# Two-layer memory attention with a SwiGLU feed-forward: GpSimd's weight sums of chunk 1, second token pair, without the wait for a copied column

## The chip, the cores and the metric

The kernel runs on one core of a Trainium2 chip. The core has engines that run at the same time, each with its own queue that is worked off in order: TensorE (PE in the profile, with its weight loads as PEld) multiplies matrices into PSUM; VectorE (DVE) and ScalarE (ACT) work element by element on SBUF and PSUM; GpSimd (POOL) does so on SBUF; SyncE (SP) issues the DMA transfers. An instruction whose operands are not ready holds up everything behind it on its engine. The metric is device time in microseconds of one execution of the whole program.

## The reference

The input x has 2048 tokens of width 512. Two layers run one after the other with the same weights. A layer is

```
x = x + A(layernorm(x))      # 32 heads of 16, four segments of 512 tokens; causal softmax attention
                             # in the segment, mixed by a gate with a linear-attention memory of the past segments
x = x + B(layernorm(x))      # B(y) = (silu(y @ w_gate) * (y @ w_up)) @ w_down, inner width 1792
```

All of it is in float32. The change touches B alone, the feed-forward part, and there only the products with w_gate and w_up.

## The kernel before, in words

*Precision.* A float32 matrix is split into a high half, which TensorE's float32 multiply takes exactly (a ScalarE copy that casts), and a low half, the rest (a subtraction). A product of two matrices is three products: high times high, low times high, high times low. So each operand that TensorE reads needs one ScalarE cast and one subtraction on VectorE or GpSimd.

*Tiling of the feed-forward.* The inner width is cut into 7 chunks of 256 (NF = 7). The 2048 tokens are four blocks of 512; the first pair of blocks is m = 0, the second m = 1. For each pair, chunk 0 is computed in the ordinary way (`up`, L1017). Chunks 1 to 6 use Strassen's method with seven products in place of eight (`strassen`, L1047), for gate (g) and up (u). It needs sums of token halves and sums of weight quarters. `down` (L1091, added to x by VectorE at L1096) multiplies the gated result by w_down. The products of gate and up are joined by `gate` and `finish` (L998, L1001, L1003, L1004).

*Token sums.* Once per pair, `make_t(m)` forms four combinations TT[0] to TT[3] of the normalised tokens, each in two k halves (kc = 0, 1), on VectorE (L961); each is split by a ScalarE cast (L982) and a VectorE subtraction (L983). The last index of a TT tile's low half, TT[2], kc = 1, is written late in that chain. The profile names its scratch tiles tt, of and xn, and the results s, which is the name of all the large SBUF slots.

*Weight sums.* `load_s(c, nm)` loads the two raw 128x512 blocks of a chunk's gate or up weights into the ring of four raw tiles phik and phiq (DMA, L858), forms four sums S1 to S4 on GpSimd (L900, 128x256 each) in the scratch tiles mem, and then splits raw quarters and sums into the weight tiles: four ScalarE casts (L913) and four GpSimd subtractions (L914), of 256, 512, 512 and 512 columns. `load_d(c)` does the same for w_down (L865, L867), without sums. Two sets of weight tiles are used in turn, so the casts of a set wait until TensorE has read the set before the last one.

*The order of the work.* The program is not issued as written. Every operation gets a priority (`at(v)`, a due time in steps of the feed-forward) and its dependencies. `Program.issue` then walks through a model of the engines: each engine takes, of the operations that are ready by the model, the one with the lowest due time. The result is one fixed order of instructions per engine. At m = 1 the due time of `load_s(1, "u")` is step 14.1 and that of `load_s(2, "g")` 14.4, those of the pair's layer norms 10.7 and 11.7, and that of `make_t(1)` 28.5.

*The turn.* `pool_turn` makes GpSimd copy one column (128x1) of a tile that another engine writes (L921). The copy waits for that writer. The GpSimd operations of a `load_s` that are given this copy as an extra dependency come behind it in the order. For chunks 2 to 6 the column is one of the gated result of block 1 of the pair. For chunk 1 of the first pair there is none. For chunk 1 of the second pair it is the last column of TT[2]'s low half, kc = 1. The list `turn` is passed to `load_s(c, "u")`, to `load_s(c + 1, "g")`, and to the last GpSimd subtraction of `load_d(c)`.

Of the kernel before, what the change touches and what calls it, by code (L numbers as in the profile page):

```python
# [253 lines left out]
def infini_swiglu(ctx: ExitStack, tc: tile.TileContext, x, wq, wk, wv, wo, beta, wg, wu, wd, out,  # L254
# [11 lines left out]
    def sb(tag, shape, dtype=F32, ring=1):  # L266
        return P.buf(pool, tag, shape, dtype, ring)
# [20 lines left out]
    def gp(cost, fn, reads, writes):  # L288
        op("pool", cost, fn, reads, writes)
# [557 lines left out]
    def ffn(base, x_in, x_out, slots, T):  # L847


        X, XT, TT, Wg, Wd = {}, {}, {}, {}, {}  # L850

        def at(v):
            P.prio = base + v * T
# [28 lines left out]
        def load_gu(tags):  # L882
            for nm, w, tag in zip("gu", (wg, wu), wset()):
                wt = Wg[0, nm] = sb(tag, [128, 2, KC, 256], F32R)
                for kp in range(2):
                    load_part(wt, kp, wsrc(w, 0, kp), tags)
# [31 lines left out]
        def pool_turn(view, read):  # L918

            one = sb("turn", [128, 1], ring=2)  # L920
            gp(0.1, lambda: nc.gpsimd.tensor_copy(one.ap, view().bitcast(F32)), [read], [one])  # L921
            return P.ops[-1:]

        def load_d(c, tags, pool=False):
            wt = Wd[c] = sb(slots[f"d{nd[0] % 2}"], [128, 2, 2, 512], F32R)
            nd[0] += 1
            for fi in range(2):
                r0 = c * 256 + fi * 128
                load_part(wt, fi, wd[r0:r0 + 128, :].rearrange("p (k f) -> p k f", k=1), tags, pool)

        def ln(b):
            XT[b] = (sb(slots[f"H{b % 2}"], TX, F32R), sb(slots[f"L{b % 2}"], TX, F32R))
            for t in range(4):
                xt = sb("xin", [128, 512], ring=2)
                load_rows(xt, x_in, b * 512 + t * 128)
                ln_transpose(ln_norm(xt, lambda a: a, None, XN2), XT[b][0], XT[b][1], t)

        def load_x(b):
            X[b] = sb(slots[f"X{b}"], [128, 4, 512])
            for t in range(4):  # L940
                r0 = b * 512 + t * 128
                dma(lambda t=t, r0=r0: nc.sync.dma_start(X[b].ap[:, t, :], rows(x_in, r0, 128)),
                    dep(x_in, r0 // 128), [(X[b], t)])
# [56 lines left out]
        def finish(sg, sv, ht, fi, pu, ru):  # L1000
            dve(512, lambda: nc.vector.tensor_mul(sv(), sv(), pu()), [sg, ru], [sg])  # L1001
            hv = lambda a: ht.ap[:, 0:2048].rearrange("p (f a c) -> p f a c", f=2, a=2)[:, fi, a]
            act(512, lambda: nc.scalar.copy(hv(0), sv()), [sg], [(ht, (fi, 0))], sbuf=True)  # L1003
            dve(512, lambda: nc.vector.tensor_sub(hv(1), sv(), hv(0).bitcast(F32)),  # L1004
                [sg, (ht, (fi, 0))], [(ht, (fi, 1))])

        def up(b, fi, ht, early):
            res = []
            for nm in "gu":
                ps = bank("pj" if early else ("plt_0", "plt_1", "plt_2", "ppv_0")[nup[0] % 4])  # L1010
                nup[0] += 1
                cs = slice(fi * 128, (fi + 1) * 128)
                first = len(P.ops)
                wt = Wg[0, nm]
                seq = [(i, j, kc) for i, j in ((0, 0), (1, 0), (0, 1)) for kc in range(KC)]
                for x, (i, j, kc) in enumerate(seq):
                    pe(512, 1, lambda i=i, j=j, kc=kc, x=x, ps=ps, wt=wt: nc.tensor.matmul(  # L1017
                        ps.ap, lhsT=wt.ap[:, i, kc, cs], rhs=XT[b][j].ap[:, :, kc], start=(x == 0),
                        stop=(x == len(seq) - 1)), [(wt, (i, kc // 2)), XT[b][j]], [ps])
                if early:  # L1020
                    P.ops[first].deps |= set(last[-1:])
                    last.append(P.ops[-1])
                res.append(ps)
            pg, pu = res
            sg = sb("raw" if early else SG, [128, 512])
            gate(sg, lambda: sg.ap, lambda: pg.ap, pg)
            finish(sg, lambda: sg.ap, ht, fi, lambda: pu.ap, pu)
# [56 lines left out]
        def down(c, b, ht):  # L1084
            for t in range(4):
                ps = bank("pj")
                cs = slice(t * 128, (t + 1) * 128)
                wt = Wd[c]
                seq = [(i, j, fi) for i, j in ((0, 0), (1, 0), (0, 1)) for fi in range(2)]
                for x, (i, j, fi) in enumerate(seq):  # L1090
                    pe(512, 1, lambda i=i, j=j, fi=fi, x=x, ps=ps, wt=wt, cs=cs: nc.tensor.matmul(  # L1091
                        ps.ap, lhsT=ht.ap[:, 0:2048].rearrange("p (f a c) -> p f a c", f=2, a=2)[:, fi, j, cs],
                        rhs=wt.ap[:, i, fi, :], start=(x == 0), stop=(x == len(seq) - 1)),
                       [(wt, (i, fi)), (ht, (fi, j))], [ps])
                xb = X[b]
                dve(512, lambda ps=ps, t=t: nc.vector.tensor_add(xb.ap[:, t, :], xb.ap[:, t, :], ps.ap),  # L1096
                    [ps, (xb, t)], [(xb, t)])
                if c == NF - 1:
                    r0 = b * 512 + t * 128
                    dma(lambda t=t, r0=r0: nc.sync.dma_start(rows(x_out, r0, 128), xb.ap[:, t, :]), [(xb, t)],  # L1100
                        [(x_out, r0 // 128)] if isinstance(x_out, Buf) else [])
# [27 lines left out]
        for m in range(2):  # L1129
            v = m * PAIR  # L1130
            if m:
                at(v - 3.0)
                load_gu(RAW)
                load_d(0, RAW)
                for b in (2, 3):
                    at(v + b - 2 - 1.2)
                    ln(b)
                    at(v + b - 2 - 1.5)
                    load_x(b)
                at(v - 0.66)  # L1140
                down(NF - 1, 0, hts[0])
                at(v + 0.33)
                down(NF - 1, 1, hts[1])
                for b in range(2):
                    hts[b] = hbuf(1 - b)
                    for fi in range(2):
                        at(v + b + 0.5 * fi)
                        up(b + 2, fi, hts[b], False)
            at(v + WAT)
            load_s(1, "g")  # L1150
            at(v + TAT[m])
            make_t(m)
            pend = (0, 1) if m else (1,)
            for c in range(1, NF):
                v = m * PAIR + 2 + (c - 1) * STEP
                at(v)
                gs = strassen(c, "g", m)
                at(v + 0.2)
                if c > 1:
                    turn = pool_turn(lambda ht=hts[1]: ht.ap[:, 1023:1024], (hts[1], (0, 1)))  # L1160
                elif m == 0:
                    turn = []
                else:
                    turn = pool_turn(lambda t=TT[2]: t.ap[:, 1, 3, 1, 127:128], (TT[2], (1, 1)))
                at(v + 0.25)
                load_s(c, "u", turn)
                if c + 1 < NF:
                    at(v + 0.55)
                    load_s(c + 1, "g", turn)
                at(v + 0.8)  # L1170
                load_d(c, RAW, True)
                P.ops[-1].deps |= set(turn)
                end = m == 1 and c == NF - 1 and not isinstance(x_out, Buf)
                before = hts
                for part in ("ud" if end else "du"):
                    at(v + (0.6 if part == "d" and not end else 1.2))
                    if part == "d":
                        for b in pend:
                            down(c - 1, b + 2 * m, before[b])
                    else:  # L1180
                        hts = {b: sb(slots[f"X{b}"], [128, 4 * 512], F32R) if end else hbuf(1 - b) for b in range(2)}
                        us = strassen(c, "u", m)
                        at(v + FIN)
                        for e in ((0, 0), (1, 1), (1, 0), (0, 1)):
                            finish(gs[0][e], gs[1][e], hts[e[1]], e[0], us[1][e], us[0][e])
                pend = (0, 1)
# [61 lines left out]
```

## Time and profile before

| | us |
|---|---|
| three runs | 1876.71, 1881.82, 1885.32 |
| their median | 1881.82 |
| the profiled execution | 1878.99 |
| its span in the profile | 1877.2 |
| TensorE busy | 1825.3 |
| VectorE busy | 1407.5 |
| GpSimd busy | 918.9 |
| ScalarE busy | 873.1 |

The profiled execution is one run of its own. Its span is the time from the first to the last instruction that the profiler recorded. Times in the profile's rows count from the start of the span. In a row of a timeline the first two numbers are the start and the duration in us, then come the engine, the line of the kernel, the operation, the tiles written and read, the shapes and the count; a bracket at the end gives the idle time of the engine before it and what ended it. A row of the windows begins with the stretch and its length and then gives the busy time and the number of instructions of PE, PEld, DVE, ACT and POOL, the clock granted to TensorE as a share of full speed, the mean busy share of the DMA engines, and GB/s.

### The profile page before, as it was taken

The numbers are of one execution on the slowest core, as the hardware profiler recorded it, in microseconds if no ns is written. First come the engines' busy times: TensorE is split into PE (matmuls) and PEld (weight loads), VectorE is DVE, ScalarE is ACT, GpSimd is POOL, SyncE is SP. The second block draws the span as 40 slices with busy tenths as digits, with TensorE's granted clock in tenths as the row PEclk, the third lists the DMA queues.
The fourth block names the chain that finished last, engine by engine and source line by source line (L and its number), as shares of the span: only waits on it lengthen the run. The fifth ranks groups of instructions, "written<-read, shape, count | busy, mean of one in ns | idle before, by whom it ended". The sixth has DMA issues, their size and how long they took to land.

```text
span 1877.2 us, 33021 instructions
## 1 busy us (share of the span) xinstructions
PE 1825.3 (97%) x11360; PEld 1450.6 (77%) x11360; DVE 1407.5 (75%) x3834; ACT 873.1 (47%) x1629; POOL 918.9 (49%) x1186
## 2 busy tenths in 40 slices
PE   7999999999999999999989999999999999999999
PEld 5787787877778887788867877778777788878887
DVE  6878788778876678766776777787898766796656
ACT  4565564555533432433345655556454433333432
POOL 6344444444655654647533444444446647445551
PEclk9999999999999999999999999999999999999999
DMA  7535444464232132111373353455642311312121
GB/s 236 148 102 147 135 133 144 144 214 119 74 119 61 46 91 89 52 50 57 114 217 101 106 163 115 130 167 140 188 124 74 123 51 56 94 64 57 44 58 45
DMA packets 126967, 206.14 MB, mean 110 GB/s; under 512 B 14160, under 2 KB 52048, under 8 KB 126800
## 3 DMA queue, kind: packets, MB, share of 16 engines
q1 hardware_dynamic: 124752, 203.49, 36.7%
q8 instruction: 91, 1.49, 0.3%
q10 hardware_dynamic: 2048, 0.53, 0.1%
q14 instruction: 76, 0.62, 0.1%
HBM read 136.34 MB, written 67.11 MB: 108 GB/s over the span
## 4 chain that ended last, share of the span: by engine, by line
PE 48%; DVE 7%; issue 2%; DMA 2%; POOL 1%; ACT 1%; SPq 0%; DVEq 0%; POOLq 0%; ACTq 0%
PE ps L1047 18%; PE ps L1091 10%; PE ps L295 7%; PE ps L636 3%; PE ps L558 3%; PE ps L609 3%; DVE junk L564 2%; DMA s<-nm 1%; PE ps L1017 1%; DVE tt L961 1%; DVE s L983 1%; DVE s L1096 1%; PE ps L387 1%; DVE mx L564 0%; DVE of L961 0%
## 5 line engine op out<-in xcount | busy, mean ns | idle before, releaser
L1047 PE MATMUL ps<-s,s 128*128 128x512 f32 x2016 | 547.3, 396 | 9.5 <-ACT s L982 4.6
L295 PE MATMUL ps<-s,s 128*128 128x512 f32 x1536 | 526.2, 407 | 2.7 <-ACT s L451 1.2
L564 DVE CUSTOM_DVE_ANT_0 junk<-ps,amask 128x128 bf16<-128x128 f32 (+3 forms) x1024 | 433.5, 484 | 46.5 <-PE ps L558 45.1
L1047 PEld LDWEIGHTS ps<-s,s 128*128 128x128 f32 x2016 | 376.7, 188 | 106.0 <-ACT s L982 6.7
L1091 PE MATMUL ps<-s,vt 128*128 128x512 f32 x1296 | 378.0, 397 | 2.2 <-ACT vt L1003 2.2
L295 PEld LDWEIGHTS ps<-s,s 128*128 128x128 f32 x1536 | 287.2, 191 | 51.6 <-issue 6.1
L615 ACT ACTIVATE s<-ps 128x512 f32<-128x512 f32 x448 | 253.9, 609 | 108.5 <-PE ps L609 97.2
L1091 PEld LDWEIGHTS ps<-s,vt 128*128 128x128 f32 x1296 | 245.2, 189 | 58.6 <-ACT vt L1003 2.6
L558 PE MATMUL ps<-ck,s 127*128 127x256 f32 (+2 forms) x1024 | 276.6, 334 | 5.7 <-DMA ck<-scrk 4.9
L609 PE MATMUL ps<-s,ck 128*128 128x256 f32 x1280 | 250.6, 287 | 6.4 <-DMA s<-nm 4.5
L609 PEld LDWEIGHTS ps<-s,ck 128*128 128x128 f32 x1280 | 221.3, 189 | 38.3 <-issue 4.9
L1096 DVE TENSOR_TENSOR s<-s,ps 128x512 f32<-128x512 f32 x224 | 150.1, 683 | 92.0 <-PE ps L1091 91.7
L619 POOL TENSOR_SCALAR_AFFINE_SELECT s<-s 128x512 f32<-128x512 f32 x192 | 126.8, 663 | 171.9 <-ACT s L615 166.6
L558 PEld LDWEIGHTS ps<-ck,s 127*128 127x128 f32 x1024 | 177.6, 189 | 28.8 <-issue 6.4
L914 POOL TENSOR_TENSOR s<-mem,s 128x512 fp32r<-128x512 f32 x96 | 130.7, 1362 | 0.0
L492 POOL TENSOR_SCALAR s<-raw 128x512 fp32r<-128x512 f32 x64 | 45.4, 709 | 173.9 <-ACT raw L491 163.6
L1017 PE MATMUL ps<-s,s 128*128 128x512 f32 x384 | 123.9, 400 | 0.9 <-ACT s L391 0.9
L921 POOL COPY turn<-vt 128x1 f32<-128x1 f32 x20 | 3.7, 186 | 235.6 <-DVE vt L1004 235.6
L636 PE MATMUL ps<-s,vt 128*32 128x384 f32 (+3 forms) x1536 | 115.7, 419 | 0.1
L636 PEld LDWEIGHTS ps<-s,vt 128*32 128x32 f32 x1536 | 43.3, 109 | 64.1 <-issue 46.2
L615 ACT ACTIVATE pc<-ps 128x512 f32<-128x512 f32 x128 | 78.7, 615 | 19.9 <-PE ps L609 19.3
L494 POOL TENSOR_TENSOR s<-raw,s 128x512 fp32r<-128x512 f32 x64 | 84.3, 1317 | 4.3
(172 smaller groups left out, 2585.3 us busy)
## 6 DMA issues: line engine op xcount, KB each, us to landing
s<-scrq SPq DMA_DIRECT2D x128, 192.0 KB, 3.5
ck<-scrk SPq DMA_DIRECT2D x128, 192.0 KB, 4.5
scrq<-s SPq DMA_DIRECT2D x32, 512.0 KB, 3.6
scrk<-s SPq DMA_DIRECT2D x32, 512.0 KB, 3.3
scrq<-s SPq DMA_DIRECT2D x32, 256.0 KB, 3.2
scrk<-s SPq DMA_DIRECT2D x32, 256.0 KB, 2.5
s<-xmid SPq DMA_DIRECT2D x32, 256.0 KB, 5.2
xin<-xmid SPq DMA_DIRECT2D x32, 256.0 KB, 2.7
```

Source lines behind the costliest of these rows:

```text
L295: pe(n, passes, lambda: nc.tensor.matmul(view(ps.ap), lhsT=av(a.ap), rhs=bv(b.ap), start=start, stop=stop), [(a, rk[0]), (b, rk[1])], [ps])
L558: nc.tensor.matmul(ps.ap[:, a * 256:a * 256 + nk], lhsT=cq.ap[0:127, 2 * j + p, qt * 128:(qt + 1) * 128], rhs=ck.ap[0:127, p, 0:nk], start ...
L564: dve(w, lambda a=a, qt=qt, w=w, ps=ps, junk=junks[qt % 2]: nc.vector.tensor_tensor_reduce(out=junk.ap[:, :w], in0=ps.ap[:, a * 256:a * 25 ...
L609: nc.tensor.matmul(ps.ap[:, 256 * p:256 * p + 256], lhsT=ck.ap[:, p, kt * 128:kt * 128 + 128], rhs=cq.ap.rearrange("r (j p) c -> r p j c", ...
L615: act(512, lambda: nc.scalar.activation(view().rearrange("p x i c -> p (x i c)"), ps.ap, AF.Exp, scale=SCALE), [ps], [(Pb, key)], table="exp")
L619: gp(0.593, lambda: nc.gpsimd.affine_select(out=view()[:, 0], in_=view()[:, 0], pattern=[[0, 4], [1, 128]], compare_op=OP.is_ge, fill=0.0, ...
L636: nc.tensor.matmul(ps.ap[32 * i:32 * i + 32, qt * 128:(qt + k) * 128], lhsT=vt.ap[:, kt, VW * hd:VW * hd + 32], rhs=view(k=k)[:, :, idx], ...
L914: gp(n / 400, lambda hi=hi, lo=lo, src=src: nc.gpsimd.tensor_sub(lo(), src(), hi().bitcast(F32)), [read, (wt, (o0, 0))], [(wt, (o0, 1))])
L1017: pe(512, 1, lambda i=i, j=j, kc=kc, x=x, ps=ps, wt=wt: nc.tensor.matmul(ps.ap, lhsT=wt.ap[:, i, kc, cs], rhs=XT[b][j].ap[:, :, kc], start ...
L1047: pe(512, 1, lambda i=i, kc=kc, x=x, buf=buf, view=view: nc.tensor.matmul(ps.ap, lhsT=w.ap[:, o, i, kc], rhs=view(buf.ap, kc), start=(x == 0),
L1091: pe(512, 1, lambda i=i, j=j, fi=fi, x=x, ps=ps, wt=wt, cs=cs: nc.tensor.matmul(ps.ap, lhsT=ht.ap[:, 0:2048].rearrange("p (f a c) -> p f a ...
L1096: dve(512, lambda ps=ps, t=t: nc.vector.tensor_add(xb.ap[:, t, :], xb.ap[:, t, :], ps.ap), [ps, (xb, t)], [(xb, t)])
```

## The change

For chunk 1 of the second pair, `turn` becomes the empty list, as it is for the first pair. The copy of TT[2]'s last column is no longer made, once in each layer. The GpSimd operations of `load_s(1, "u")` and `load_s(2, "g")` and the last subtraction of `load_d(1)` have only their own data dependencies left. All else is as it was, the turns of chunks 2 to 6 too.

```
                 if c > 1:
                     turn = pool_turn(lambda ht=hts[1]: ht.ap[:, 1023:1024], (hts[1], (0, 1)))
-                elif m == 0:
+                else:
                     turn = []
-                else:
-                    turn = pool_turn(lambda t=TT[2]: t.ap[:, 1, 3, 1, 127:128], (TT[2], (1, 1)))
                 at(v + 0.25)
                 load_s(c, "u", turn)
                 if c + 1 < NF:
```

More of the change, by code (lines that the diff above doesn't have):

```diff
@@ L1160, in ffn @@
                     turn = pool_turn(lambda ht=hts[1]: ht.ap[:, 1023:1024], (hts[1], (0, 1)))
-                elif m == 0:
+                else:
                     turn = []
-                else:
-                    turn = pool_turn(lambda t=TT[2]: t.ap[:, 1, 3, 1, 127:128], (TT[2], (1, 1)))
                 at(v + 0.25)
```

## The prediction

> **What bounds the kernel.** I read the page's first part, then TensorE's waits around the two places where the changed copy runs, then the granted clock there, then each engine's timeline.
>
> ```profile
> span 1877.2 us, 33021 instructions
> PE 1825.3 (97%) x11360; PEld 1450.6 (77%) x11360; DVE 1407.5 (75%) x3834; ACT 873.1 (47%) x1629; POOL 918.9 (49%) x1186
> ...
> L921 POOL COPY turn<-s x2: 581/882/1182, 746.4 to 1675.1; 128x1 f32<-128x1 f32 x2
> ...
> 751.76 0.73 PE L1047 MATMUL ps<-s,s 128*128 128x512 f32 x1 [3.15 <-POOL s L914]
> ...
> 753.62 0.79 PE L1047 MATMUL ps<-s,s 128*128 128x512 f32 x1 [0.70 <-ACT s L982]
> ...
> 1682.15 0.50 PE L1047 MATMUL ps<-s,s 128*128 128x512 f32 x1 [2.56 <-ACT s L982]
> ...
> 1684.91 0.80 PE L1047 MATMUL ps<-s,s 128*128 128x512 f32 x1 [0.26 <-DVE s L983]
> ...
> 750.00:754.00 4.00, 1.53 (x3) 0.82 (x4) 3.97 (x5) 2.28 (x4) 4.00 (x4) 0.73 0.25 66
> 754.00:758.00 4.00, 4.00 (x10) 3.09 (x10) 2.89 (x4) 1.03 (x2) 4.00 (x4) 0.50 0.23 65
> 758.00:762.00 4.00, 4.00 (x17) 3.25 (x16) 3.45 (x5) 1.31 (x3) 4.00 (x5) 0.91 0.00 1
> ...
> 1680.00:1684.00 4.00, 1.85 (x7) 1.52 (x8) 3.97 (x5) 2.38 (x4) 4.00 (x3) 0.96 0.18 66
> 1684.00:1688.00 4.00, 3.75 (x11) 2.55 (x10) 2.43 (x4) 0.00 (x0) 4.00 (x5) 0.61 0.23 70
> ...
> 775.00:890.00 115.00, 115.00 (x498) 93.02 (x498) 74.97 (x115) 44.65 (x78) 66.94 (x75) 1.00 0.17 50
> ```
>
> TensorE is busy 97% of the span, so a microsecond lost or won on it is one of the end time unless a later stall swallows it; after the first place it runs 115 us without a gap (last row). The copy that goes runs twice, at 746.4 us (layer 0) and 1675.1 us (layer 1). Near it TensorE stands still for 3.15 + 0.70 us and for 2.56 + 0.26 us. In the window rows the last three columns are granted clock, DMA share and GB/s: behind each stall the clock is halved for a while. Taking the missing clock of each row over one half, that lasted (0.27 + 0.50 + 0.09) x 4 / 0.5 = 6.9 us in layer 0 and (0.04 + 0.39) x 4 / 0.5 = 3.4 us in layer 1, a loss of 3.4 and 1.7 us.
>
> Behind whom the releasers stood:
>
> ```profile
> 746.44 1.18 POOL L921 COPY turn<-s 128x1 f32<-128x1 f32 x1 [3.87 <-DVE s L983]
> ...
> 752.43 0.62 ACT L913 CAST s<-mem 128x512 fp32r<-128x512 f32 x1 [0.69 <-POOL mem L900]
> 752.96 0.61 ACT L982 CAST s<-of 128x512 fp32r<-128x512 f32 x1
> ...
> 1680.96 0.62 ACT L913 CAST s<-mem 128x512 fp32r<-128x512 f32 x1 [1.65 <-POOL mem L900]
> 1681.49 0.61 ACT L982 CAST s<-of 128x512 fp32r<-128x512 f32 x1
> ```
>
> In layer 0 the first stall is for the low half of the weights of u, chunk 1 (GpSimd L914). In both layers the next is for the high half of a token sum (`of`, TT[1]), whose ScalarE cast L982 stands in order behind the cast L913 of a weight sum (`mem`) that GpSimd had not finished. GpSimd itself had sat idle 3.87 us for the column (746.44). So the wait does cost something today. The last stall, 1684.91, is for VectorE's low half L983.
>
> ```profile
> 742.68 0.68 DVE L961 TENSOR_TENSOR tt<-tt,s 128x512 f32<-128x512 f32 x1
> ...
> 747.50 0.68 DVE L1096 TENSOR_TENSOR s<-s,ps 128x512 f32<-128x512 f32 x1
> ...
> 750.03 1.09 DVE L961 TENSOR_TENSOR of<-of,s 128x512 f32<-128x512 f32 x1
> ...
> 1673.12 1.28 DVE L961 TENSOR_TENSOR tt<-s,s 128x512 f32<-128x512 f32 x2
> 1674.33 0.68 DVE L983 TENSOR_TENSOR s<-xn,s 128x512 fp32r<-128x512 f32 x1
> 1674.93 0.68 DVE L961 TENSOR_TENSOR tt<-tt,tt 128x512 f32<-128x512 f32 x1
> 1675.53 0.68 DVE L1001 TENSOR_TENSOR raw<-raw,ps 128x512 f32<-128x512 f32 x1
> ...
> 1676.83 1.23 DVE L983 TENSOR_TENSOR s<-tt,s 128x512 fp32r<-128x512 f32 x1
> 1677.98 1.22 DVE L1004 TENSOR_TENSOR vt<-raw,vt 128x512 fp32r<-128x512 f32 x1
> 1679.13 1.22 DVE L961 TENSOR_TENSOR of<-of,s 128x512 f32<-128x512 f32 x1
> ...
> 1683.08 1.77 DVE L983 TENSOR_TENSOR s<-of,s 128x512 fp32r<-128x512 f32 x1
> 1684.78 0.68 DVE L1096 TENSOR_TENSOR s<-s,ps 128x512 f32<-128x512 f32 x1
> ...
> 1675.62 0.74 POOL L900 TENSOR_TENSOR mem<-phiq,phiq 128x256 f32<-128x256 f32 x1
> ...
> 1682.58 1.73 POOL L914 TENSOR_TENSOR s<-phiq,s 128x512 fp32r<-128x512 f32 x1
> ```
>
> This fence carries the forecast. VectorE's token-sum operations start 0.60 us apart (1674.33, 1674.93, 1675.53) while GpSimd waits for the copied column. Once GpSimd's weight work begins (1675.62) they start 1.15 apart (1676.83, 1677.98, 1679.13): 0.55 more beside a 256-column operation, and 1.10 more beside a 512-column one (1683.08 to 1684.78, next to L914 at 1682.58). Operations with one operand in PSUM (`ps`: L1001, L1096) stay at 0.68. It looks as if the two engines take turns, one operation each. The copied column keeps most of GpSimd's work out of VectorE's chain.
>
> By the Trainium skill, page "SBUF — State Buffer", section "Who interferes with whom", a VectorE instruction with two SBUF inputs contends with a GpSimd instruction that reads SBUF and the one that comes second is blocked fully; the trace agrees, 0.60 against 1.15 us. Read as a whole-instruction block it would charge GpSimd's undisturbed length, which the L900 row gives as 0.74 us, where the spacing shows 0.55; with the nine turns of layer 0 below, five of them short, that would add about 1.0 us there.
>
> **The change, part by part.**
>
> *Removed.* One 128x1 copy per layer, 1.18 and 0.58 us of GpSimd (L921), and its wait. GpSimd is busy 49%; the copy itself is worth nothing.
>
> *Moved, the four sums of u, chunk 1 (L900).* They need only the two raw blocks and the `mem` scratch, and their priority (14.1 steps of the second pair) goes ahead of all but the layer norms. So they go behind the previous set's L914 operations, long before:
>
> ```profile
> 695.16 0.97 SPq L858 DMA_DIRECT2D phik<-in_B_w_up_dram  x2
> ...
> 702.42 1.29 POOL L914 TENSOR_TENSOR s<-mem,s 128x512 fp32r<-128x512 f32 x1
> ...
> 716.80 1.74 POOL L914 TENSOR_TENSOR s<-mem,s 128x512 fp32r<-128x512 f32 x1
> 721.62 1.96 POOL L379 TENSOR_SCALAR xn<-xin,brs 128x512 f32<-128x512 f32 x2 [3.07 <-PE ps L387]
> ```
>
> The raw blocks were issued at 695.16. Two sums fit behind 702.42, two behind 716.80, 0.74 us each. They are queued ahead of layer-norm steps, which may come 1.5 us later, but the next layer-norm operation (721.62) sits idle 3.07 us for TensorE: covered. Without that cover the second batch's transposes would be up to 1.5 us late. Layer 1 has the same order.
>
> *Moved, four L914, the sums of g, chunk 2, and two L867.* The L914 now wait only for ScalarE's casts of the weights, which start when the weight tile is free, at 739.99 and 1673.05:
>
> ```profile
> 739.99 0.40 ACT L913 CAST s<-phik 128x256 fp32r<-128x256 f32 x1
> ...
> 741.71 0.86 POOL L370 TENSOR_TENSOR brs<-bmv,mhalf 128x1 f32<-128x1 f32 x1
> ...
> 1673.05 0.39 ACT L913 CAST s<-phiq 128x256 fp32r<-128x256 f32 x1
> ```
>
> In layer 0 they stand behind a layer-norm step that ends at 742.57. So GpSimd's run of work begins near 742.57 in place of 746.44, and near 1673.46 in place of 1675.07, and starts with the 512-column L914 in place of 256-column sums. The DMAs of the w_down blocks follow the freed raw tiles and so come earlier; SP has no other transfer waiting behind them at these places, and their landing ends no stall of TensorE today. g of chunk 2 still waits for its tile (freed by TensorE): nothing.
>
> *What VectorE pays, layer 0.* From 742.68 to the end of `of` there are 12 operations, 10 of them SBUF only. Undisturbed: 742.68 + 12 x 0.60 = 749.88 (today about 751.1, so the delay today is 1.2). Nine turns of GpSimd fall between: L914 of 256 (0.55), L914 of 512 (1.10), a sum (0.55), two L914 (2.20), three sums (1.65), one L867 (1.10), together 7.15; the two PSUM operations hide 0.60 each. So 749.88 + 5.95 = 755.83, then the cast at once (0.05 + 0.62) and 0.04: TensorE resumes at 756.54, not 753.62: **+2.9 us**. The 3.15 us stall for L914 goes; behind it TensorE has two matmuls and then waits for `of`, which is late next.
>
> *Layer 1.* From 1673.12 there are nine operations, one PSUM: undisturbed end 1678.52. Seven turns (0.55, 1.10, 0.55, 1.10, 1.10, 0.55, 0.55 = 5.50) less 0.60: 1683.42, against 1680.35 today. Cast and start: 1684.1, against 1682.15. Then four operations (2.40) and three more turns (0.55 + 1.10 + 1.10 - 0.60 = 2.15) to the low half: 1687.97, start at 1688.0 against 1684.91: **+3.1 us**.
>
> Sum +6.0 us. *Bounds.* If a 512-column turn costs only the 0.55 of a short one: layer 0 4.95 - 1.2 = 3.75, +0.7; layer 1 `of` at 1681.77, low half 3.45 later, +0.4; together +1.1. At the other end the longer stalls each add one slow-clock stretch like that of layer 1 (1.7 us): +9.4. I take +6.0, nearest to the 1.70 spacing that the trace shows, and no change of clock loss, since layer 0's stretch could also shorten.
>
> By the Trainium skill, "TensorE: Matmul & The Clock Gate", Part 1, the clock halves after an idle window of about 3.4 us and returns after a busy one; the 6.9 and 3.4 us above look like two windows and one. By it the stalls forecast here, 7.4 and 4.5 us, would be at the upper end.
>
> The profiled execution took 1878.99 us (span 1877.2); the median of the runs shown is 1881.82, 2.8 higher. Against its own time: 1878.99 + 6.0 = 1885.0 us.
>
> **Rivals.**
>
> *Faster: VectorE keeps its pace and GpSimd yields.* Then `of` ends at 749.88 and 1678.52, the cast no longer stands behind a sum, TensorE waits from 749.1 to 750.6 and not at all in layer 1. Saved: 3.0 + 2.8 us of stalls, and with them the slow stretches, 3.4 + 1.7: 1878.99 - 10.9 = 1868.1. For it: GpSimd's rows stretch as well (1.73 for L914). Against: VectorE's spacing above. It decides where `of` comes later by less than 1.8 us in layer 0 (751.1 to 752.96 is what ScalarE's order costs today); with `of` exactly as today only that order is saved, 1.8 us in layer 0 and 1.1 in layer 1, 1876.1.
>
> *Small or nothing.* The short turns of the lower bound: released casts and lost turns nearly cancel, +1.1, 1880.1. For it: the long turn rests on one clean spacing. The change not doing what it says would land here too: if the casts, not the copy, held GpSimd back; against, GpSimd's 3.87 us of idle time before 746.44, with a cast done at 740.39.
>
> *Slower by more.* One more slow stretch per layer, 1878.99 + 9.4 = 1888.4. For it: both stalls grow past 4 us. Against: in layer 0 the clock was already low for 6.9 us.
>
> **How the numbers follow.** Chances: forecast 0.45, slower by more 0.24, small or nothing 0.19, faster 0.12. The range takes 1875 (between "small" and the faster end) to 1894 (the upper end with the 0.3% by which the runs shown differ), leaving out about 2 in 10. Half a per cent, 9.4 us, is about what a measurement of this kernel can tell from no change: faster than that 0.05 (part of the faster rival), slower 0.27 (most of "slower by more", the top of the forecast), the rest 0.68.
>
> **What would show it.** GpSimd's L900 sums of `mem<-phik` near 704 and 719, and its L914 near 743; no stall of L1047 on POOL L914, but one on ACT L982 of about 7 us in layer 0, and on L982 and L983 of about 4.5 and 2 us in layer 1; VectorE's L961 and L983 at 1.2 to 1.8 us from 742 on. It is wrong if these stay at 0.68, or if TensorE's later work shows new stalls.

## The result, and the profile after

The changed kernel took 1882.2 us in the median (1876.87 to 1889.54, 22 runs) where the kernel before, run beside it, took 1880.13 us (22 runs, of which one took 4466.44 us and is left out of the ratio). The ratio is 1.0013, with a 95% interval of 1.0004 to 1.0022: about 2.4 us slower, within the half per cent that was called no change. The profiled execution took 1879.36 us. The forecast was 6.0 us, 2.9 in layer 0 and 3.1 in layer 1.

```profile
span 1877.6 us, 33020 instructions
PE 1825.2 (97%) x11360; PEld 1450.9 (77%) x11360; DVE 1409.8 (75%) x3834; ACT 872.0 (46%) x1629; POOL 918.4 (49%) x1184
```

The page's totals hardly move, so the two places have to be measured on their own. The copied columns that the change leaves alone serve as markers: the stretch of a layer runs from the column of the last chunk of the first token pair to that of chunk 2 of the second pair. Here they are in GpSimd's timeline of the kernel after (start in us, duration, engine and line).

```profile
677.94 0.18 POOL L921 COPY turn<-vt 128x1 f32<-128x1 f32 x1 [11.52 <-DVE vt L1004]
785.64 0.18 POOL L921 COPY turn<-vt 128x1 f32<-128x1 f32 x1 [11.11 <-DVE vt L1004]
...
1612.16 0.18 POOL L921 COPY turn<-vt 128x1 f32<-128x1 f32 x1 [11.18 <-DVE vt L1004]
1745.15 0.18 POOL L921 COPY turn<-vt 128x1 f32<-128x1 f32 x1 [13.47 <-DVE vt L1004]
```

That is 107.70 us in layer 0 and 132.99 us in layer 1. Before, the same markers stood 104.83 us (678.07 to 782.90) and 133.23 us (1611.51 to 1744.74) apart. **So layer 0 grew by 2.87 us, as forecast, and layer 1, which was to grow by 3.1, did not grow (-0.24).** The same code gives these stretches to between 0.3 and 0.7 us: layer 1 is unchanged in l0_only below and took 132.91 for 133.23, and its changed layer 0 took 108.35 for 107.70; layer 0 is unchanged in l1_only and took 104.44 for 104.83, and its changed layer 1 took 132.51 for 132.99. The -0.24 lies inside that scatter.

**Layer 0.** VectorE's timeline of the kernel after:

```profile
745.40 1.23 DVE L961 TENSOR_TENSOR tt<-s,s 128x512 f32<-128x512 f32 x1
746.55 0.68 DVE L1001 TENSOR_TENSOR raw<-raw,ps 128x512 f32<-128x512 f32 x1
...
748.26 1.76 DVE L983 TENSOR_TENSOR s<-xn,s 128x512 fp32r<-128x512 f32 x1
749.94 1.21 DVE L1004 TENSOR_TENSOR vt<-raw,vt 128x512 fp32r<-128x512 f32 x1
...
752.21 0.68 DVE L1096 TENSOR_TENSOR s<-s,ps 128x512 f32<-128x512 f32 x1
...
755.21 1.63 DVE L961 TENSOR_TENSOR of<-of,s 128x512 f32<-128x512 f32 x1
```

The turns have the forecast price: 745.40 to 746.55 is 1.15 beside a short operation of GpSimd, 748.26 to 749.94 is 1.68 beside a long one, and the operations with `ps` stay at 0.68. `of` ends at 756.84 (forecast 755.83). GpSimd's side, and TensorE's waits in both layers:

```profile
703.65 0.73 POOL L900 TENSOR_TENSOR mem<-phik,phik 128x256 f32<-128x256 f32 x1
...
719.54 0.73 POOL L900 TENSOR_TENSOR mem<-phik,mem 128x256 f32<-128x256 f32 x1
721.50 0.77 POOL L379 TENSOR_SCALAR xn<-xin,brs 128x512 f32<-128x512 f32 x1 [1.23 <-PE ps L387]
...
742.42 0.73 POOL L914 TENSOR_TENSOR s<-phik,s 128x256 fp32r<-128x256 f32 x1
...
1674.17 2.68 POOL L914 TENSOR_TENSOR s<-phiq,s 128x256 fp32r<-128x256 f32 x1 [16.51 <-ACT s L913]
```

```profile
752.94 2.07 PE L1091 MATMUL ps<-s,vt 128*128 128x512 f32 x4 [3.94 <-DVE s L1096]
757.55 0.80 PE L1047 MATMUL ps<-s,s 128*128 128x512 f32 x1 [2.54 <-ACT s L982]
...
1678.49 3.38 PE L1091 MATMUL ps<-s,vt 128*128 128x512 f32 x14
...
1687.28 0.79 PE L1047 MATMUL ps<-s,s 128*128 128x512 f32 x1 [2.85 <-DVE s L983]
```

TensorE resumes the products on `of` at 757.55 (forecast 756.54). It stood 3.94 + 2.54 = 6.48 us, where before it stood 3.85: 2.63 of the 2.87 us. But the forecast had one wait of about 7 us. In fact TensorE first waited for L1096, the addition that frees a bank of the down product: it has an operand in PSUM and pays no turn itself, but it stands in VectorE's queue behind operations that do. It then had four matmuls to do before the wait for `of`.

The granted clock (third column from the right) of the kernel after:

```profile
750.00:754.00 4.00, 1.06 (x3) 0.88 (x4) 3.97 (x6) 1.10 (x2) 4.00 (x4) 0.72 0.00 0
754.00:758.00 4.00, 1.46 (x4) 0.73 (x3) 3.97 (x5) 0.75 (x2) 2.30 (x2) 0.50 0.36 86
758.00:762.00 4.00, 4.00 (x11) 3.03 (x11) 3.68 (x8) 0.62 (x1) 0.00 (x0) 0.50 0.13 46
...
1684.00:1688.00 4.00, 1.15 (x4) 0.63 (x3) 4.00 (x4) 0.00 (x0) 3.80 (x4) 0.88 0.37 114
1688.00:1692.00 4.00, 4.00 (x14) 3.16 (x13) 3.02 (x5) 1.73 (x3) 1.28 (x1) 0.70 0.01 2
```

In layer 0 the slow clock lasts (0.28 + 0.50 + 0.50) x 4 / 0.5 = 10.2 us, one stretch of 3.4 more than before. It costs little, since TensorE stands for 2.54 us of the window 754 to 758 anyway: stalls alone make 2.63 of the 2.87. In layer 1 it lasts (0.12 + 0.30) x 4 / 0.5 = 3.4 us, as before.

**Layer 1.** VectorE's timeline of the kernel after, at the second place:

```profile
1673.77 1.28 DVE L961 TENSOR_TENSOR tt<-s,s 128x512 f32<-128x512 f32 x2
1674.97 0.68 DVE L983 TENSOR_TENSOR s<-xn,s 128x512 fp32r<-128x512 f32 x1
1675.57 0.68 DVE L961 TENSOR_TENSOR tt<-tt,tt 128x512 f32<-128x512 f32 x1
1676.18 0.68 DVE L1001 TENSOR_TENSOR raw<-raw,ps 128x512 f32<-128x512 f32 x1
...
1677.49 1.68 DVE L961 TENSOR_TENSOR of<-of,s 128x512 f32<-128x512 f32 x1
...
1686.01 1.21 DVE L983 TENSOR_TENSOR s<-of,s 128x512 fp32r<-128x512 f32 x1
```

Two things differ from what was forecast. GpSimd's first low half (1674.17 above) lasts 2.68 us in place of 0.74, and beside it VectorE keeps 0.60 from operation to operation: here GpSimd yields. And the order is another one: the last step of `of` (1677.49) now comes ahead of L983 on `tt` and of L1004, behind which it stood before, TensorE has 14 matmuls of the down product in hand (1678.49), and between `of` and its low half (1686.01) VectorE now has L1004, three L1096 and the L983 on `tt` to do. Which of the two spared layer 1 had to be tried.

### The profile page after: what moved, and what is told of

It is laid out like the page before. It is cut to its first block, busy times and chain, and to the rows that moved or that the text cites. A ratio compares the mean times of both kernels' runs of the same rounds, so it can differ in the third digit from the quotient of the medians.

```text
span 1877.6 us, 33020 instructions
## 1 busy us (share of the span) xinstructions
PE 1825.2 (97%) x11360; PEld 1450.9 (77%) x11360; DVE 1409.8 (75%) x3834; ACT 872.0 (46%) x1629; POOL 918.4 (49%) x1184
## 4 chain that ended last, share of the span: by engine, by line
PE 75%; DVE 13%; issue 5%; DMA 4%; POOL 2%; ACT 2%; SPq 1%; DVEq 0%; POOLq 0%; ACTq 0%
PE ps L1047 24%; PE ps L295 14%; PE ps L1091 14%; PE ps L558 6%; PE ps L636 6%; PE ps L609 6%; DVE junk L564 3%; PE ps L1017 3%; PE ps L387 1%; DVE s L983 1%; DVE tt L961 1%; DVE mx L564 1%; DMA s<-nm 1%; DMA ck<-scrk 1%; DVE s L1096 1%
## 5 line engine op out<-in xcount | busy, mean ns | idle before, releaser
L1047 PEld LDWEIGHTS ps<-s,s 128*128 128x128 f32 x2016 | 377.0, 188 | 103.2 <-ACT s L982 5.2
L295 PEld LDWEIGHTS ps<-s,s 128*128 128x128 f32 x1536 | 286.8, 190 | 51.6 <-issue 6.1
L1096 DVE TENSOR_TENSOR s<-s,ps 128x512 f32<-128x512 f32 x224 | 149.8, 682 | 89.2 <-PE ps L1091 89.0
L1017 PEld LDWEIGHTS ps<-s,s 128*128 128x128 f32 x384 | 71.6, 188 | 19.3 <-ACT s L391 1.9
```

The costliest lines, as they stand in the source:

```text
L295: pe(n, passes, lambda: nc.tensor.matmul(view(ps.ap), lhsT=av(a.ap), rhs=bv(b.ap), start=start, stop=stop), [(a, rk[0]), (b, rk[1])], [ps])
L1047: pe(512, 1, lambda i=i, kc=kc, x=x, buf=buf, view=view: nc.tensor.matmul(ps.ap, lhsT=w.ap[:, o, i, kc], rhs=view(buf.ap, kc), start=(x == 0),
```

## The experiments

All stretches, with the ratio of times to the kernel before in the same comparison:

| kernel | layer 0, us | layer 1, us | ratio [95% interval] |
|---|---|---|---|
| before | 104.83 | 133.23 | 1 |
| after | 107.70 | 132.99 | 1.0013 [1.0004, 1.0022] |
| l0_only | 108.35 | 132.91 | 1.0019 [1.0005, 1.0032] |
| l1_only | 104.44 | 132.51 | 0.9994 [0.9980, 1.0009] |
| sums_free | 105.95 | 135.95 | 1.0040 [1.0028, 1.0052] |
| write_only | 103.64 | 128.77 | one time, 1873.93 us |
| order_kept | 106.62 | 130.73 | 0.9993 [0.9981, 1.0004] |
| l1_kept | 104.81 | 130.69 | 0.9990 [0.9979, 1.0001] |
| late_start | 106.40 | 130.78 | 1.0006 [0.9996, 1.0016] |
| psum_start | 106.14 | 130.74 | 0.9999 [0.9990, 1.0008] |
| later_start | 106.26 | 130.71 | 1.0003 [0.9989, 1.0016] |
| late3 | 105.84 | 130.99 | 0.9999 [0.9989, 1.0009] |
| late1 | 106.32 | 132.48 | 1.0003 [0.9990, 1.0016] |
| two_turns | 103.84 | 134.76 | 1.0039 [1.0023, 1.0054] |

### One layer at a time: l0_only and l1_only

```
-                elif m == 0:
+                elif m == 0 or isinstance(x_out, Buf):        # l0_only
+                elif m == 0 or not isinstance(x_out, Buf):    # l1_only
```

> The change in layer 0 alone; layer 1 keeps the copied column. Theory (VectorE's token sums pay for GpSimd's earlier work): the stretch from the copied column of the first pair's last chunk (678 us in the profile before) to that of the second pair's chunk 2 (783 us) takes 107.7 us as in the changed kernel, against 104.8 before, +2.9; layer 1's stretch between its copied columns, 1611.5 to 1744.7 us in the profile before, stays at 133.2. Rival (the delay is given back in layer 1's attention, where the changed kernel took 2.1 us less between 909 and 1489 us): the same stretches, but the attention between them about 2 us shorter than before, and the end within 1 us of the kernel before. Without that give-back the end is 2.9 us later, a ratio of 1.0015.

> The change in layer 1 alone; layer 0 keeps the copied column. Theory: nothing in layer 0 (104.8 us between the copied columns), -0.2 us in layer 1 (133.0 us), ratio 0.9999. Rival (layer 1 was spared by chance, GpSimd yielding its turns to VectorE in that one execution): up to +3.1 us, 136.3 us, ratio 1.0016, with the cast L982 of the token sum `of` ending the wait of TensorE as in layer 0.

Both came out as the theory had it: 108.35 us in layer 0 for the first, 132.51 us in layer 1 for the second. The layers do not answer alike, and the second result is not the chance of one execution: freeing the work in layer 1 costs nothing. The stretch between the markers of the two layers (layer 1's attention) took 581.63 us in l0_only and 581.73 in l1_only, 582.71 before and 580.60 after, with the same order of work; over all the kernels of the table it lies between 580.60 (after) and 586.70 (l1_kept). Nothing shows that time is given back there.

### What GpSimd's reads cost: write_only

The changed kernel; the four low halves of u, chunk 1, of the second pair are left out and two blanks each are written in their place. It ran once. (Its lines after 913 stand up to 5 further down: L987 and L988 are L982 and L983.)

```
...
+                    if blank:
+                        nc.gpsimd.memset(lo().bitcast(F32), 0.0)
+                        nc.gpsimd.memset(lo().bitcast(F32), 0.0)
+                    else:
+                        nc.gpsimd.tensor_sub(lo(), src(), hi().bitcast(F32))
...
```

> The changed kernel, with the four GpSimd subtractions L914 of u, chunk 1, second pair, each replaced by two memsets of the same output: they read nothing from SBUF. The low halves of these weights are left out of the result. The order on TensorE, VectorE and ScalarE is that of the changed kernel. Theory (GpSimd's reads hold up VectorE's operations with two SBUF inputs, 0.55 us a short and 1.10 us a long one): VectorE is spared 3.85 us before the end of `of` in layer 0, so TensorE resumes about 3.9 us earlier than in the changed kernel, near 753.7 us in place of 757.5, and the layer 0 stretch takes 102 to 104 us in place of 107.7. Rival (the order of VectorE's and ScalarE's work, not the reads, made the delay): VectorE's spacing stays at 1.15 to 1.7 us beside the memsets and the stretch at 107.7.

Layer 0 fell to 103.64 and layer 1 to 128.77, 4.1 and 4.2 us less than in the kernel after. Its timelines, GpSimd and then VectorE, over the same two microseconds:

```profile
746.30 0.52 POOL L916 MEMSET s<- 128x512 f32 x1
746.88 0.53 POOL L917 MEMSET s<- 128x512 f32 x1
```

```profile
746.27 0.68 DVE L988 TENSOR_TENSOR s<-tt,s 128x512 fp32r<-128x512 f32 x1
746.88 0.68 DVE L988 TENSOR_TENSOR s<-xn,s 128x512 fp32r<-128x512 f32 x1
747.48 0.68 DVE L1009 TENSOR_TENSOR vt<-raw,vt 128x512 fp32r<-128x512 f32 x1
```

Beside work of GpSimd that only writes, VectorE keeps 0.60. It is GpSimd's reads, not its being busy, that VectorE pays for, and that the turns are what delays layer 0 is shown (4.1 us for four low halves, where their turns were put at 3.85). The Trainium skill, page "SBUF — State Buffer", section "Who interferes with whom", says the same: a VectorE instruction with two SBUF inputs contends with a GpSimd instruction that reads SBUF, not with one that only writes it.

### Only the sums free: sums_free

The kernel before, in which only the four sums of u, chunk 1, lose the column; the low halves keep it.

```
-                P.ops[-1].deps |= set(after)
+                P.ops[-1].deps |= set(after if sums is None else sums)
...
-                load_s(c, "u", turn)
+                load_s(c, "u", turn, () if c == 1 else None)    # the sums' own list of what they wait for
```

> Only the four sums of u, chunk 1 (L900) lose the copied column; the subtractions L914 and what comes behind still wait for it. Theory (the column costs ScalarE's order, the early L914 cost VectorE): the casts of the sums no longer block ScalarE, and GpSimd's four short turns are gone from VectorE's chain, so TensorE's stalls get shorter by 1 to 2 us in each layer: 103.3 to 104 us in layer 0, end 2 to 3 us earlier than before, ratio 0.9985 to 0.999. Rival (the wait for L914's low half keeps the end of the stall where it is, 751.7 us): unchanged within 0.5 us in layer 0, ratio 1.000.

It missed: 1.0040, and 1.1 and 2.7 us more in the two stretches. VectorE's timeline shows why:

```profile
750.12 1.66 DVE L961 TENSOR_TENSOR of<-s,tt 128x512 f32<-128x512 f32 x1
751.82 1.64 DVE L961 TENSOR_TENSOR of<-of,s 128x512 f32<-128x512 f32 x1
...
758.11 1.74 DVE L983 TENSOR_TENSOR s<-of,s 128x512 fp32r<-128x512 f32 x1
```

With the sums gone, GpSimd works on the low halves, three of the four long, as soon as it has the column, and long ones meet both steps of `of`, where before short operations had stood (1.10 there). Then sums and L867 meet the low half of `of`. Taking turns away ahead of a critical operation moves worse ones onto it. The two stretches account for 3.8 us of the 7.5 that 0.40% makes. VectorE's order shifted elsewhere too: in layer 1 the first two chunks of the first pair took 30.34 and 30.63 us in place of 29.99 and 29.90, and with three chunks of layer 0 that is 1.8 us more. Where the rest lies was not followed.

### The wait alone, with the old order: order_kept and l1_kept

The copy of the column stays in the plan, with all its dependences, so the written order of every engine is that of before (the trace has the same sequence of operations on TensorE, VectorE and ScalarE); but what it copies is a column of a weight tile that has long been written. l1_kept does this in layer 1 alone.

```
-                    turn = pool_turn(lambda t=TT[2]: t.ap[:, 1, 3, 1, 127:128], (TT[2], (1, 1)))
+                    turn = pool_turn(lambda t=Wg[1, "g"][0]: t.ap[:, 0, 0, 0, 0:1], (TT[2], (1, 1)))
```

> The kernel before, in which the copied column is taken from a weight tile that has long been written, so that the copy waits for nothing, while the order of the instructions on TensorE, VectorE, ScalarE and GpSimd stays that of before. So only the wait goes, and not the order. If the forecast failed in layer 1 because the freed order was another one there, then under the old order its sum holds: the low halves of u, chunk 1, start near 1673.5 us, `of` ends near 1683.4, and the stretch of layer 1 between its markers grows from 133.2 to about 136.3 us; in layer 0 it grows from 104.8 to about 107.5; ratio to before about 1.003. If GpSimd simply yields to VectorE in layer 1 (its first low half took 2.7 us in the changed kernel while VectorE kept 0.60), layer 1 stays within 0.6 us of 133.2 and the ratio is about 1.0014.

> The kernel before, in which the copied column of layer 1 alone is taken from a weight tile long written; the order of the instructions stays that of before. Layer 0 has nothing changed and stays at 104.8 us (0.7 either way), layer 1 falls from 133.2 to 130.7 as in order_kept, so 1876.5 beside the 1879 of before: ratio 0.9987 (0.998 to 0.9995). If the 130.7 was chance, the ratio is 1.000.

Layer 0 grew to 106.62 (expected 107.5), and **layer 1 fell to 130.73 us: not +3.1 but -2.5.** Neither of the two expectations for layer 1 held; the second had the mechanism, and missed its size. l1_kept gave 130.69, with 104.81 in layer 0 and a ratio of 0.9990, all as expected, and the three kernels below that keep the same code in layer 1 gave 130.71 to 130.78. GpSimd's timeline of order_kept, between its markers in layer 1:

```profile
1611.33 0.18 POOL L921 COPY turn<-vt 128x1 f32<-128x1 f32 x1 [11.31 <-DVE vt L1004]
...
1673.52 2.70 POOL L914 TENSOR_TENSOR s<-phiq,s 128x256 fp32r<-128x256 f32 x1 [14.04 <-ACT s L913]
1676.18 3.05 POOL L900 TENSOR_TENSOR mem<-phiq,mem 128x256 f32<-128x256 f32 x1
...
1742.06 0.18 POOL L921 COPY turn<-vt 128x1 f32<-128x1 f32 x1 [12.69 <-DVE vt L1004]
```

Its VectorE and TensorE there, and the granted clock:

```profile
1677.34 0.67 DVE L1004 TENSOR_TENSOR vt<-raw,vt 128x512 fp32r<-128x512 f32 x1
1677.94 0.68 DVE L961 TENSOR_TENSOR of<-of,s 128x512 f32<-128x512 f32 x1
1678.65 1.12 DVE L961 TENSOR_TENSOR tt<-s,of 128x512 f32<-128x512 f32 x1
...
1681.38 1.77 DVE L983 TENSOR_TENSOR s<-of,s 128x512 fp32r<-128x512 f32 x1
```

```profile
1680.45 0.50 PE L1047 MATMUL ps<-s,s 128*128 128x512 f32 x1 [1.04 <-ACT s L982]
...
1683.21 0.50 PE L1047 MATMUL ps<-s,s 128*128 128x512 f32 x1 [0.64 <-DVE s L983]
```

```profile
1680.00:1684.00 4.00, 2.91 (x11) 2.10 (x12) 3.75 (x4) 1.53 (x3) 4.00 (x3) 1.00 0.11 11
1684.00:1688.00 4.00, 4.00 (x19) 3.27 (x18) 3.29 (x5) 1.11 (x2) 4.00 (x5) 1.00 0.16 58
```

GpSimd's first two reading operations take 2.70 and 3.05 us, and beside them VectorE goes on at 0.60 until `of` ends at 1678.62, 1.7 us before the 1680.35 of before. TensorE stands 1.04 + 0.64 = 1.68 us in place of 2.82, and the clock does not drop: 1.1 + 1.7 = 2.8 us, for the 2.5 measured. The clock agrees in direction only with the Trainium skill, page "TensorE: Matmul & The Clock Gate", Part 1, which lets it drop after an idle window of about 3.4 us: the short stalls here cost no slow stretch, but in the kernel before a stall of 2.56 us, less than such a window, was enough for one.

**So the wait's removal is worth -2.5 us in layer 1 if the order is kept, and the order that came with the change gives 2.3 back** (132.99 - 130.73). That is the whole order of all four engines; that it goes through the low half of `of` is read from the rows, not tried by itself: 1686.01 against 1681.38, at markers 0.83 us apart, and the 2.85 us that TensorE waits for it at 1687.28, with the slow clock behind. Of the 2.3 us TensorE's standing still makes 1.2 (2.85 against 1.68); the rest goes to the slow stretch. In layer 0 the same comparison reads: the wait alone, with the old order, costs 1.8 us (106.62 against 104.83), and the order that came with the change another 1.1 (107.70 against 106.62).

### When GpSimd starts: late_start, psum_start, later_start

Why does GpSimd yield in layer 1 and not in layer 0? All three are order_kept with blanks written by GpSimd, in layer 0, ahead of its first sum (blanks cost VectorE nothing, above): two of 128x256 in late_start, one of 128x256 and three of 128x512 in psum_start, three of 128x256 in later_start. The edit of late_start:

```
-                gp(0.65, lambda: getattr(nc.gpsimd, f)(out(), x(), y()), reads, [w_])
+                gp(0.65, lambda: ([nc.gpsimd.memset(out(), 0.0) for _ in range(2)] if late and w_ == (m[0], 1) else [], getattr(nc.gpsimd, f)(out(), x(), y())), reads, [w_])
```

> The kernel with the old order and no wait for the column (order_kept), in which in layer 0 GpSimd writes two blanks of 128x256 into the scratch of the first sum of u, chunk 1, before that sum. Blanks took 0.31 us each and VectorE kept 0.60 beside them. So GpSimd's first reading instruction starts near 742.5 and not at 741.9 us, inside VectorE's unbroken run of token sums and not at its pause. If the engine that is under way keeps its pace until it has an operation with a PSUM operand or a gap (as in layer 1 of order_kept, where the low half took 2.70 us and VectorE kept 0.60), then VectorE now keeps 0.60 in layer 0 too until about 747 us, `of` ends near 750.5 in place of 753.87, and the stretch of layer 0 falls from 106.6 to 103.5 to 104.8 us; layer 1 stays at 130.7; ratio to before 0.998 (0.9975 to 0.9990). If the moment of the start plays no part, VectorE's spacing is 1.15 from 742.5 on and the stretch stays at 106.6.

> As late_start, with one blank of 128x256 and three of 128x512 (some 2.1 us), so that GpSimd's first sum starts near 744.0 us, while VectorE is in L1001, whose second operand lies in PSUM. If the engine under way keeps its pace, GpSimd is the one under way when L1001 ends, and VectorE pays a turn from its next operation on: spacing 1.15 from 744.4 us, `of` ends near 752.5 to 753.5, stretch of layer 0 105.5 to 106.5 us, longer than in late_start although GpSimd starts 1.5 us later. If a later start of GpSimd simply takes turns away from VectorE, the stretch is shorter than in late_start.

> As late_start, with three blanks of 128x256 in place of two, so that GpSimd's first reading instruction in layer 0 starts some 0.35 us later: about 0.45 to 0.5 us after the start of VectorE's operation under way, where it was 0.11 us after it. In the traces so far every GpSimd read that started up to 0.24 us into a VectorE operation with both operands in SBUF made VectorE's next such operation wait (1.2 to 1.8 us), and every first one that started 0.39 to 0.48 us into it did not, and took 2.0 to 2.7 us itself. If that moment decides, VectorE now keeps 0.60 from one operation to the next in layer 0 up to L1096, GpSimd's first sums take 1.4 us and 3 us, `of` ends some 3 us earlier relative to the copy than in late_start, and the stretch of layer 0 falls from 106.4 to 103 to 105 us; ratio to before 0.998 to 0.999. If the moment within the operation plays no part (what differs between the layers is the kind of instruction, the low half L914 in layer 1 and a sum L900 in layer 0), VectorE waits as in late_start, 1.23 us from its third operation on, and the stretch stays at 106 to 107 us, ratio 1.000.

Layer 0 took 106.40, 106.14 and 106.26 us, where order_kept has 106.62: the start makes no difference that these stretches can tell, and the theory that the engine under way keeps its pace fell with late_start, in its finer form with later_start. psum_start's 106.14 lies inside its expectation, but it was to be longer than late_start and is not. In later_start, GpSimd and then VectorE:

```profile
744.90 0.80 POOL L900 TENSOR_TENSOR mem<-phik,phik 128x256 f32<-128x256 f32 x1
```

```profile
744.41 0.69 DVE L961 TENSOR_TENSOR xn<-xn,xn 128x512 f32<-128x512 f32 x1
745.01 1.23 DVE L961 TENSOR_TENSOR tt<-s,s 128x512 f32<-128x512 f32 x1
```

GpSimd starts 0.49 us into VectorE's operation, later than in layer 1 (1673.52, with VectorE's operation begun at 1673.13 in order_kept, so 0.39), and VectorE still waits at its next one. The 0.49 lies just beyond the starts at which GpSimd yielded (0.39 to 0.47 in the traces), so a narrow window of the moment is made unlikely by it, not ruled out. What is left is this: in layer 1 VectorE had run for over 20 us without a pause (in order_kept from 1651.33 on, 22.2 us), in layer 0 it had paused 0.8 to 6.6 us before every start that made it wait. That fits all starts in the traces that fell on two operations of VectorE with both operands in SBUF and no gap between them, but it also separates the two layers, and no run takes them apart. **Which of the two engines yields, and why, stays open.** Kernels that start GpSimd in layer 0 only after a longer run of VectorE, or at another moment in layer 1, were not run.

### Fewer turns: late3, late1, two_turns

Three ways to leave fewer reads of GpSimd beside `of`. late3 and late1 are the changed kernel with a new column, of TT[3] or of TT[1], for the sums of g, chunk 2, and for the second of the two L867 (the dependence that the code has reaches only the last one, so the first stays free, against what the expectation says). two_turns is sums_free with the column of TT[3] for that later work.

```
                 load_s(c, "u", turn)
+                if m and c == 1:
+                    turn = pool_turn(lambda t=TT[3]: t.ap[:, 1, 3, 1, 127:128], (TT[3], (1, 1)))
```

> The changed kernel, in which only the eight operations for u, chunk 1, stay free, while the sums of g, chunk 2, and the two L867 wait for a column of the last token sum, TT[3]. The order on VectorE and ScalarE stays nearly that of the changed kernel. Beside `of` four turns are left in layer 0 (0.55 + 3 x 1.10 = 3.85 us) where there were nine: `of` ends near 753.7 in place of 756.8 us, and the stretch of layer 0 falls from 107.7 to about 104.5; layer 1 from 133.0 to about 131.5. Ratio to before 0.9985 (0.9975 to 0.9995). If the turns are not what delays VectorE, the stretches stay at 107.7 and 133.0 and the ratio at 1.001.

> As the kernel that holds the sums of g, chunk 2, and the two L867 until a column of TT[3], but until one of TT[1] (`of`), which is written some microseconds earlier. `of` ends as there; the operations of VectorE behind it meet the sums and L867 again, so its stretches lie between: layer 0 near 105.5, layer 1 near 132; ratio to before 0.999.

> The four sums of u, chunk 1, are free; its four low halves wait for the column of TT[2] as before; the sums of g, chunk 2, and the two L867 wait for a column of TT[3]. The low halves still meet `of` (the kernel that freed the sums alone lost 1.1 and 2.7 us), but the low half of `of` behind them no longer stands beside sums and L867, which cost 2.97 and 3.15 us of waiting there. So about 1.5 us less per layer than that kernel: layer 0 near 104.5, layer 1 near 134; ratio to before 1.000 to 1.002.

In layer 0 the direction was right and the size short: late3 takes 1.9 us off the kernel after there, not 3.2. With 2.0 off in layer 1 it stands level with the kernel before (0.9999, expected 0.9985). One of the missing turns is the L867 that stayed free; in the timelines of late3 it meets L1004:

```profile
750.09 1.57 POOL L867 TENSOR_TENSOR s<-phik,s 128x512 fp32r<-128x512 f32 x1 [0.71 <-ACT s L865]
```

```profile
750.46 1.75 DVE L1004 TENSOR_TENSOR vt<-raw,vt 128x512 fp32r<-128x512 f32 x1
```

late1 lies above late3 in both layers, as expected, but the 0.5 us of layer 0 are no more than the scatter, and the 1.5 us of layer 1 are not the turns'. TensorE's waits in layer 1, late3 and then late1, and the clock of late1:

```profile
1687.30 0.50 PE L1047 MATMUL ps<-s,s 128*128 128x512 f32 x1 [2.29 <-DVE s L983]
```

```profile
1691.20 0.69 PE L1047 MATMUL ps<-s,s 128*128 128x512 f32 x1 [2.35 <-DVE s L983]
```

```profile
1692.00:1696.00 4.00, 4.00 (x13) 3.11 (x13) 2.35 (x4) 1.58 (x3) 3.85 (x5) 0.66 0.00 0
```

The waits are nearly the same, 2.29 and 2.35 us, but the clock drops behind the second and stays at 1.00 behind the first. Nor do the turns explain the 2.0 us of layer 1 between late3 and the kernel after: `of` ends 67.0 us and its low half starts 73.8 us behind the first marker in both, so the turns taken away saved nothing at these two. The 2.0 us are 0.6 less of waiting (2.29 for 2.85) and the slow stretch that did not come. In l1_only it did come, behind a wait of 2.32 us. So where TensorE waits about 2.3 us, whether the clock drops makes some 1.5 us of difference between these stretches (130.99 against 132.51 and 132.48).

two_turns hit its stretches (103.84 and 134.76, expected 104.5 and 134) and still took 0.39% more, 7.3 us in four runs: its two stretches add 0.5 us, chunks elsewhere about 1.8 as in sums_free, and where the rest lies was not followed. No version is faster than the kernel before beyond its interval; l1_kept, 0.9990 [0.9979, 1.0001], comes nearest.

## Why the prediction was right or wrong

- **The time.** The sum, +6.0 us, was too high by 3.6; +2.4 lies inside the range and inside the half per cent, and the forecast's sign was right. The layer 1 half of the sum never came, so that the sign was right rests on layer 0 alone. The "small or nothing" rival's number, +1.1, was nearer (1.3 off), but not its reason: a long turn costs its full 1.10 in layer 0 (1.68 from 748.26 to 749.94).
- **The moved sums**: right. They run at 703.65 to 719.54, and the layer-norm step behind them still waits for TensorE (1.23 us at 721.50, of 3.07).
- **GpSimd's start in layer 0**: right, 742.42 for 742.57. It began with the 256-column low half, as the sum of turns had it, not with a 512-column one, as the sentence ahead of the sum says.
- **"What VectorE pays, layer 0", +2.9**: right in its mechanism, and +2.87 in the time. That the two agree so closely is luck: ends and stalls were about 1 us off, in opposite directions (TensorE resumed at 757.55 for 756.54, and stood 6.48 us for 7.4), and one wait was not foreseen: L1096, which pays no turn itself, came late behind operations that did. write_only shows that the reads are the cause; order_kept shows that 1.1 of the 2.87 came only with the new order. "No change of clock loss" was wrong by the length of the slow stretch, but what it added fell mostly on time in which TensorE stood.
- **"Layer 1", +3.1: this step failed.** It carried the turns of layer 0 over to layer 1, "Seven turns", and there VectorE paid none at first. The rival "VectorE keeps its pace and GpSimd yields" held in layer 1 alone: with the order kept the stretch fell by 2.5 us. Its price there had been put at 2.8 us of stalls and 1.7 of slow clock; the slow clock went, the stalls shrank by 1.1.
- **"Layer 1 has the same order"**: wrong as well, and it hid the first error. The sentence was written for the sums and taken over for everything. Once sums and low halves were free, ScalarE's and VectorE's written order changed, and the new order cost 2.3 us of the 2.5. Two errors of opposite sign left -0.24, by luck.
- **What it said would make it wrong**, VectorE's operations staying at 0.68, is what layer 1 showed, in the first four.

## What to carry to other kernels

A price read in one place of a trace holds for the state the engines are in there: before it is used in a second place, look for a row of that place that shows it. Where a planner writes the order, removing a dependence is two changes, the wait and the order; keep the dependence in the plan and empty it in the program, and each can be timed alone. And a wait that keeps a reading engine away from a critical chain should be judged by which of its reads would land on which operation of that chain, not by how long the engine stands idle.

## What the runs showed that was not expected

- GpSimd's first read of 256 columns in layer 1 took 2.68 to 2.70 us in nine kernels with either order, beside three or more operations of VectorE at 0.60, and the sum behind it 3.04 to 3.05 us wherever the old order was kept; undisturbed, such an operation takes 0.73 or 0.74. The Trainium skill, page "SBUF — State Buffer", section "Who interferes with whom", lets whoever issues first hold the shared port for the whole instruction; the turns of layer 0 look like that, but here GpSimd, already waiting, did not get its turn at the end of VectorE's instruction, nor at the next ones.
- In order_kept it got in at an operation with a PSUM operand (its first read ends with L1001, at 1676.22) and at a pause of 0.03 us (1678.62 to 1678.65), behind which the two engines took turns again.
- In the kernel after, the slow-clock time of layer 0 grew by a stretch of 3.4 us and cost next to nothing, since TensorE stood through part of it. In layer 1 of order_kept the same length went, worth up to 1.7 us (half of 3.4), and a wait of TensorE of 2.29 us brought no such stretch where one of 2.32 did.
